# Spectral branch over the sequence in two halves, with seven more buffer pairs and runs of 13 key tiles

## The chip, the core and the metric

The kernel runs on one core of a Trainium2 chip. A core has a matrix engine (TensorE, PE in the profile, with PEld for its weight loads), a vector engine (VectorE, DVE), an activation engine (ScalarE, ACT), GpSimd (POOL) and SyncE (SP). Here SP computes nothing: it issues every DMA of the kernel, one after the other, and waits in its own order for what each DMA needs. The metric is the device time of one execution in microseconds (us). The kernel before took 1010.61 us, the median of three runs (1010.15 to 1011.03).

## The reference

Two independent branches read inputs of 2048 tokens by 448 features and are joined along the features, everything in float32:

```
a = einsum("bsd,ed->bse", x, dft_hid_re)
b = einsum("bsd,ed->bse", x, dft_hid_im)
y = einsum("ts,bse->bte", dft_seq_re, a) - einsum("ts,bse->bte", dft_seq_im, b)     # spectral branch
...
qkv = x @ wqkv                       # 16 heads of 28
p = softmax(q k^T * scale)
attention = (p v) @ wo
out = concatenate([y, attention])
```

The spectral branch is a transform along the features (448 by 448 matrices) and then one along the sequence (two 2048 by 2048 matrices). The attention branch is full softmax attention with 16 heads.

## The kernel before, in words

**Precision.** Most operands are split in two parts, a rounded high part and the rest (names ending in h and l, or hi and lo). A product is then three matmuls (high by high, low by high, high by low). ACT makes the high part, POOL or DVE the low part by a subtraction.

**The planner.** No order is written out by hand. The kernel describes tasks (`sch.add`, with helpers `pe`, `act`, `dve`, `pool`, `dma`) with an engine, a key (a due time in us), dependencies and the buffers they take; `Schedule.run` then plays through a modelled clock. Whenever an engine is free in the model it picks the ready task with the lowest key, and the instruction is emitted in that order. So the order on each engine is fixed when the kernel is built. On the chip an engine waits if its next instruction is not ready. The model of a DMA is in lines 284 to 291: besides fixed latencies, transfers pass one after another through a pipe of `FLOW_IN` = 310 (GB/s) in the first 20 us of the model (`T_IN`) and of `FLOW` after that (line 68), and at most eight DMAs are in flight (`LANES`).

**Fill and attention.** PE's work has two streams. The *fill* stream is a chain in a fixed order with two PSUM banks (`NFILL`): the projections of q and k (line 581 through `project`), the values (line 581 through `values`), the hidden transform (`hidden`, line 581 with weights in wd), and the sequence transform (`sequence`, line 718). Its keys (`fkey`) spread it evenly from the start to `T_FILL` = 1005. The *attention* stream takes the other six banks: for each head and each of 16 key tiles four score matmuls (line 865), each followed by an exponential on ACT (line 869) into half of a buffer *pair*. Its keys run from `T_ATT` = 56 to `T_END` = 935, so a key tile is due every 879 / 256 = 3.434 us. A head's first key tile has its own path (`first_tiles`, lines 806 to 839).

**Runs.** Exponentials times values (line 848, four matmuls for a key tile side by side in four groups of 32 columns) are not done one key tile at a time: `sums` gathers `run_size` key tiles, and when the exponentials of all of them are there PE does the whole run without a break. All pairs of the run stay taken until then: two pairs for each key tile. `RUN_AT` gives runs of 8 key tiles before a due time of 230 us and of 10 from there. Counted with 3.434 us for a key tile from 56 us, that is 7 runs of 8 (56 key tiles) and 20 of 10.

**Buffers.** `kept` holds 22 pairs of 4 KB for each partition. Three more are *lent* to it: they live in the place of a weight tile (tag wd) while no weights are there. A `Weights` object takes these three places back: from a due time on (`lent.until`, 50 us before the key of the hidden transform that needs the weights) nothing is lent any more, and the weights are converted into the place when the last lent pair is free. `big` is one tile of 57 KB for each partition. It holds x of the attention branch, split, until the last projection; then the spectral branch's a, split, for all 16 token tiles, and later -b in the same place.

**The spectral branch before.** `hidden(0)` makes a for all 16 token tiles (16 times 11 matmuls), `sequence(0)` multiplies dft_seq_re with it: 16 output tiles, each a sum over all 16 token tiles in one bank (48 matmuls, four pieces of dft_seq of 256 KB). DVE copies each result out (line 732), and it is stored to `y_d` in device memory. `hidden(1)` and `sequence(1)` do the same with b; here the stored y is loaded (line 735) once the third of the four pieces has begun (`Q_YO` = 2), DVE adds (line 736), and the sum is stored to `out`.

**The end.** After the last run, `out_of` normalises the last head through small DMAs to memory and back, the output projection (line 1003) follows in four chunks of 44 matmuls, copied out at line 431 and stored at line 1011. The rest of the fill runs beside it.

## Time and profile before

| | |
|---|---|
| median of three runs | 1010.61 us |
| profiled execution, its own time | 1010.71 us |
| span of its trace, first to last instruction | 1008.9 us |
| time outside the span | 1.81 us |
| ACT busy | 712.3 us (71%) |
| POOL busy | 366.9 us (36%) |
| DVE busy | 319.8 us (32%) |
| bytes moved by DMA | 124.84 MB |
| matmul records of line 718, line 581 with 448 columns, line 865, line 848 | 1536, 528, 960, 2048 |

A profile line such as `L848 PE MATMUL bank<-kept,v ... x64` names the line of the kernel, the engine, the operation, what is written and read, and the number of instructions. The matmuls of line 848 have float32 operands and leave two records each, so a key tile is eight records. Matmuls overlap: the duration of one record is longer than the step from one to the next, so the pace is read from the starts.

### The profile page before, as it was taken

Reading aid. Unit: us, or ns where it says so; the run is one execution under the profiler, and the core shown is the slowest. Engines: PE = TensorE matmul, PEld = TensorE weight load, DVE = VectorE, ACT = ScalarE, POOL = GpSimd, SP = SyncE. Lnnn points to the kernel's source line nnn. Section 1 sums busy time; section 2 is a strip of 40 time slices with the busy share of each in tenths; the row PEclk is TensorE's granted clock in tenths of the full one; section 3 lists DMA queues with packets and bytes.
Section 4 is the critical chain, followed back from the end, with each engine's and each line's share of the span. In section 5 each row is a group of like instructions: output and inputs, shape, how many; then the busy total and the mean of one; then the engine's idle time right before and its main releaser. Section 6 shows DMA issues by size and latency. Waiting matters only on the chain.

```text
span 1008.9 us, 15993 instructions
## 1 busy us (share of the span) xinstructions
PE 1001.6 (99%) x5634; PEld 735.3 (73%) x5634; DVE 319.8 (32%) x608; ACT 712.3 (71%) x1410; POOL 366.9 (36%) x338
## 2 busy tenths in 40 slices
PE   8999999999999999999999999999999999999998
PEld 7896667777766876686668667766786677667797
DVE  6362525251515042412314051614042152300112
ACT  6117979788767866796679778877786687668242
POOL 5112234353324323442325443434334252444530
PEclk9999999999999999999999999999999999999999
DMA  9797464323233333333233424332433343233463
GB/s 327 226 163 205 127 188 150 98 76 114 69 102 102 112 96 106 97 106 102 80 111 110 132 71 119 93 112 80 148 98 100 117 141 105 70 123 117 139 187 130
DMA packets 109908, 124.84 MB, mean 124 GB/s; under 512 B 48640, under 2 KB 61440, under 8 KB 109824
## 3 DMA queue, kind: packets, MB, share of 16 engines
q1 hardware_dynamic: 109824, 123.78, 40.8%
q8 instruction: 45, 0.74, 0.3%
q14 instruction: 39, 0.32, 0.1%
HBM read 89.92 MB, written 33.69 MB: 123 GB/s over the span
## 4 chain that ended last, share of the span: by engine, by line
PE 98%; DVE 1%; DMA 1%; SPq 0%; issue 0%; DVEq 0%
PE bank L718 31%; PE bank L865 23%; PE bank L848 22%; PE bank L581 17%; PE bank L1003 4%; PE bank L806 1%; DMA kept<-xb 1%; DVE big L427 0%; SPq L488 0%; SPq L559 0%; DVE kept L598 0%; DVE kept L736 0%; DVEq L427 0%
## 5 line engine op out<-in xcount | busy, mean ns | idle before, releaser
L869 ACT ACTIVATE kept<-bank 128x512 f32<-128x512 f32 x944 | 509.4, 673 | 90.7 <-PE bank L865 87.6
L530 POOL TENSOR_TENSOR wlo<-wraw,whi 128x512 fp32r<-128x512 f32 (+1 forms) x164 | 202.9, 1237 | 471.4 <-ACT whi L524 397.1
L865 PE MATMUL bank<-q,k 98*128 98x512 f32 x960 | 329.4, 398 | 0.0
L718 PE MATMUL bank<-big,whi 128*128 128x448 f32 x1024 | 310.9, 367 | 0.0
L848 PE MATMUL bank<-kept,v 128*32 128x512 f32 x2016 | 224.4, 593 | 0.0
L718 PEld LDWEIGHTS bank<-big,whi 128*128 128x128 f32 x1024 | 193.3, 189 | 29.2 <-issue 3.4
L865 PEld LDWEIGHTS bank<-q,k 98*128 98x128 f32 x960 | 180.4, 188 | 44.2 <-issue 11.7
L718 PE MATMUL bank<-big,wlo 128*128 128x448 f32 x512 | 188.3, 368 | 0.0
L848 PEld LDWEIGHTS bank<-kept,v 128*32 128x32 f32 x2016 | 63.5, 110 | 144.4 <-issue 142.3
L524 ACT ACTIVATE whi<-wraw 128x512 fp32r<-128x512 f32 x164 | 113.8, 694 | 21.0 <-PE bank L718 17.0
L718 PEld LDWEIGHTS bank<-big,wlo 128*128 128x128 f32 x512 | 96.7, 189 | 16.9 <-issue 5.9
L837 POOL TENSOR_TENSOR kept<-kept,mb 128x512 f32<-128x512 f32 x54 | 79.5, 1473 | 62.9 <-DVE mb L832 27.5
L581 PE MATMUL bank<-wd,whi 128*128 128x448 f32 x256 | 79.8, 367 | 0.0
L811 DVE STREAM_TRANSPOSE mb<-bank 128x512 f32<-128x512 f32 x64 | 45.8, 715 | 101.6 <-PE bank L806 87.9
L839 ACT ACTIVATE kept<-kept 128x512 f32<-128x512 f32 x64 | 45.1, 772 | 33.3 <-POOL kept L837 29.9
L581 PE MATMUL bank<-big,whi 128*128 128x512 f32 x175 | 60.1, 394 | 0.2 <-DVE kept L598 0.2
L832 DVE STREAM_TRANSPOSE mb<-am 128x512 f32<-128x512 f32 x64 | 45.4, 710 | 41.1 <-POOL kept L837 39.9
L810 ACT ACTIVATE kept<-bank 128x512 f32<-128x512 f32 x64 | 41.6, 672 | 22.5 <-PE bank L806 21.6
L581 PEld LDWEIGHTS bank<-wd,whi 128*128 128x128 f32 x256 | 48.3, 189 | 6.1 <-issue 0.8
L894 ACT ACTIVATE kept<-bank 128x512 f32<-128x512 f32 x16 | 9.5, 597 | 55.1 <-PE bank L848 55.1
L776 DVE TENSOR_REDUCE ok<-v 128x1 f32<-128x512 f32 x16 | 11.0, 686 | 115.5 <-DMA v<-vd 115.4
L736 DVE TENSOR_TENSOR kept<-bank,kept 128x448 f32<-128x448 f32 x15 | 9.3, 623 | 120.2 <-PE bank L718 106.0
(74 smaller groups left out, 745.8 us busy)
## 6 DMA issues: line engine op xcount, KB each, us to landing
wraw<-wre SPq DMA_DIRECT2D x64, 256.0 KB
wraw<-wim SPq DMA_DIRECT2D x64, 256.0 KB
qkd<-kept SPq DMA_DIRECT2D x40, 256.0 KB
wraw<-xa SPq DMA_DIRECT2D x32, 256.0 KB
k<-qkd SPq DMA_DIRECT2D x64, 112.0 KB
q<-qkd SPq DMA_DIRECT2D x64, 112.0 KB
out<-kept SPq DMA_DIRECT2D x31, 224.0 KB
kept<-xb SPq DMA_DIRECT2D x16, 256.0 KB
```

What stands on the lines that cost most here:

```text
L524: a = act(key + (0 if early else 1), lambda: nc.scalar.activation(self.hi.t, raw.t, AF.Copy), ACT_S, soon=SOON, deps=[ld], acq=[self.hi], ...
L530: b = sch.add(e, at, lambda g: eng[g].tensor_tensor(self.lo.t[:, :n], raw.t[:, :n], f32(self.hi.t)[:, :n], op=ALU.subtract), deps=[a], acq ...
L581: nc.tensor.matmul(o.t[:, :cols], w(), x(), start=(i == 0), stop=(i == n - 1))
L718: nc.tensor.matmul(o.t[:, :D], a.t[:, k, :], b[:, q * 4 + k, :], start=(q == 0 and k == 0 and j == 0), stop=(q == 3 and k == 3 and j == 2))
L810: made.append(act(key, lambda o=o, s=s: nc.scalar.activation(s.t, o.t, AF.Copy), deps=[m], use=[o, s.pair], lock=[o]))
L811: t = dve(key, lambda o=o, tm=tm: nc.vector.transpose(tm.t, o.t), 0.73, deps=[m], acq=[tm], use=[o], lock=[o], own=RAW_S)
L832: t = dve(key, lambda mb=mb, c=c: nc.vector.transpose(mb.t, f32(am.t)[:, c * NT:(c + 1) * NT].unsqueeze(2).to_broadcast([P, NT, 32])), 0.7 ...
L837: sh = sch.add({"DVE": 0.8, "POOL": POOL_2}, key, lambda e, s=s, mb=mb: eng[e].tensor_tensor(s.t, s.t, mb.t, op=ALU.add), deps=[t, made[c] ...
L839: shown.append(act(key, lambda s=s: nc.scalar.activation(s.t, s.t, AF.Exp, scale=SCALE), ACT_S, deps=[sh], use=[s.pair]))
L848: nc.tensor.matmul(o.t[c * VW:(c + 1) * VW, :], VT[h].t[:, kt // 4, kt % 4, :], tiles[c].t, start=(kt == 0), stop=(kt == NT - 1))
L865: m = pe(key, lambda e, o=o, q=q, kt=kt: nc.tensor.matmul(o.t, KT[h][kt // 4].t[:KM, kt % 4 * P:(kt % 4 + 1) * P], q.t[:KM, :], start=True ...
L869: es[h, kt].append(act(key - 20, lambda o=o, p=p: nc.scalar.activation(p.t, o.t, AF.Exp, scale=SCALE), deps=[m], use=[o, p.pair]))
```

## The change

The tokens of the spectral branch are taken in two halves of eight tiles. `big` becomes two tiles x0 and x1 of half its size, split by tokens. `hidden` and `sequence` run four times instead of twice: (part a, first half), (a, second half), (b, first), (b, second). The order of the hidden transform's 32 token tiles is the same; the sequence transform makes each of its 16 output tiles four times, each time from eight token tiles (24 matmuls, two pieces of 256 KB). a and -b of a half fit in x0 alone. The first of the four passes stores y by a copy as before, the second and third load y, add and store it again, the fourth loads, adds and stores to `out`. The load may now go out once the second of two pieces has begun (`Q_YO` = 1).

The hidden transform needs its weights four times. The first set is the held one as before; the other three are loaded and split anew, each taking the lent places back 50 us before its key.

x1 is free after the last projection. Its 28 KB hold seven more pairs (`more`, `held`), which join `kept` when the last matmuls that read x have been done: 29 pairs, and three lent ones.

`RUN_AT` changes to runs of 8 before 200 us and of 13 from there: 6 runs of 8 (48 key tiles) and 16 of 13. `FLOW` in the planner's model of a DMA goes from 200 to 300.

```diff
--- before.py
+++ after.py
@@ -34,10 +34,10 @@
 NKEPT = 22
 NKEYS = 4
 NFILL = 2
-Q_YO = 2
+Q_YO = 1
 N_WARM = 7
 N_FIRST = 3
-RUN_AT = ((0.0, 8), (230.0, 10))
+RUN_AT = ((0.0, 8), (200.0, 13))
 
 
 def run_size(t):
@@ -65,7 +65,7 @@
 RAW = 0.19
 RAW_S = 0.12
 LANES = 8
-FLOW, FLOW_IN = 200.0, 310.0
+FLOW, FLOW_IN = 300.0, 310.0
 T_IN = 20.0
 FIRST = {"PE": 1.4, "ACT": 2.0, "DVE": 2.0, "POOL": 1.4, "SP": 0.75}
 FLOW_AT = 1.4
@@ -355,7 +355,8 @@
     on_d = dram.tile([D, S], F32, name="ond")
 
 
-    big = new("big", [P, 2 * NT * D], F32R)
+    SIDE = 7 * S // 2
+    xs = [new(f"x{i}", [P, SIDE], F32R) for i in range(2)]
     lent = Lent(lambda: sb.tile([P, 2 * 4 * D], F32R, tag="wd", name="wd"),
                 lambda: [t[:, i] for t in (sb.tile([P, 3, 2, CH], F32, tag="wd", name="lent"),) for i in range(3)], 3)
     wraw = new("wraw", [P, 4, P], F32, 3, True)
@@ -377,6 +378,16 @@
     w_first.part(0)
     stage_s = Slots([w_first.tile[:, i * CH:(i + 1) * CH] for i in range(7)])
     kept_s.lent = lent
+    more, N_MORE = [], SIDE // (2 * CH)
+
+    def place_of(i):
+        if not more:
+            more.append(sb.tile([P, N_MORE, 2, CH], F32, tag="x1", name="more"))
+        return more[0][:, i]
+    held = [Slot(kept_s) for _ in range(N_MORE)]
+    for i, slot in enumerate(held):
+        slot.i = len(kept_s.tiles)
+        kept_s.tiles.append(lambda i=i: place_of(i))
     fill_s, bank_s = Slots(banks[:NFILL]), Slots(banks[NFILL:])
 
     class Half:
@@ -459,17 +470,23 @@
         return at + (f - HEAD) * (T_FILL - at) / (F_TOTAL - HEAD)
 
 
+    def x_part(i, s):
+        side, at = divmod(s.start, S // 2)
+        at += i * S // 2
+        return xs[side][:, at:at + s.stop - s.start]
+
     def x_h(k, s):
-        return big[:, k * S + s.start:k * S + s.stop]
+        return x_part(k, s)
 
     def x_l(k, s):
-        return big[:, (3 + k) * S + s.start:(3 + k) * S + s.stop]
+        return x_part(3 + k, s)
 
     def x_3(s):
-        return big[:, 6 * S + s.start:6 * S + s.stop]
-
-    ab_h = big[:, :NT * D].rearrange("p (t d) -> p t d", t=NT)
-    ab_l = big[:, NT * D:].rearrange("p (t d) -> p t d", t=NT)
+        return x_part(6, s)
+
+    NS = NT // 2
+    ab_h = xs[0][:, :NS * D].rearrange("p (t d) -> p t d", t=NS)
+    ab_l = xs[0][:, NS * D:].rearrange("p (t d) -> p t d", t=NS)
 
 
     def products(xh, xl, x3, wh, wl):
@@ -644,7 +661,8 @@
             pair = None if st else kept_s.slot()
             hi, lo = (stage_s.slot(), stage_s.slot()) if st else (Half(pair, 0), Half(pair, 1))
             own = [hi, lo] if st else [pair]
-            end = chain(key, seq, o, CH, [], w.own if first else [w.hi, w.lo], M512, own, parts)
+            end = chain(key, seq, o, CH, [], w.own if first else [w.hi, w.lo], M512,
+                        [*own, *(held if j == 6 and c == NC - 1 else ())], parts)
             key, out_key = (0.0, 11.0 if j == 0 else 25.0) if first else (key - 10, key - 10)
             stored(j, c, o, end, own, hi, lo, st, key, out_key)
         x_users.append(last[0])
@@ -663,7 +681,7 @@
                 seq = products(lambda k: lz(x_h, k, tok), lambda k: lz(x_l, k, tok), lambda: lz(x_3, tok),
                                lambda k: (lambda: w_first.h[:, k]), lambda k: (lambda: w_first.l[:, k]))
                 key = fkey(11, M448)
-                end = chain(key, seq, o, D, [], [], M448, [pair],
+                end = chain(key, seq, o, D, [], [], M448, [pair, *(held if c == NC - 1 and t == 3 else ())],
                             {3 * k: [xb_ready[c, k], ready[k], *ready[4:][:k // 3]] for k in range(4)}, v_last)
 
                 def put(o=o, vs=vs):
@@ -679,16 +697,16 @@
 
     y_stored = {}
 
-    def hidden(part, weights, ready, after):
+    def hidden(part, half, weights, ready, after):
         done = []
-        for st in range(NT):
+        for st in range(half * NS, (half + 1) * NS):
             key = fkey(11, M448)
             w = Piece(lambda st=st: xa[st], key - 9, "x")
             o = fill_s.slot()
             seq = products(lambda k, w=w: (lambda: w.hi.t[:, k]), lambda k, w=w: (lambda: w.lo.t[:, k]),
                            lambda w=w: (lambda: w.hi.t[:, 3]), lambda k: (lambda: weights.h[:, k]), lambda k: (lambda: weights.l[:, k]))
-            end = chain(key, seq, o, D, [*w.ready, *ready], [w.hi, w.lo], M448, weights.slots if st == NT - 1 else ())
-            hi, lo = ab_h[:, st, :], ab_l[:, st, :]
+            end = chain(key, seq, o, D, [*w.ready, *ready], [w.hi, w.lo], M448, weights.slots if st % NS == NS - 1 else ())
+            hi, lo = ab_h[:, st % NS, :], ab_l[:, st % NS, :]
             if part == 0:
                 a = act(key - 10, lambda o=o, hi=hi: nc.scalar.activation(hi, o.t[:, :D], AF.Copy), 0.43, soon=SOON, deps=[end, *after], use=[o])
                 b = dve(key - 10, lambda o=o, hi=hi, lo=lo: nc.vector.tensor_tensor(
@@ -701,22 +719,23 @@
             done.append(b)
         return done
 
-    def sequence(part, made):
+    def sequence(part, half, made):
         src = wim if part else wre
+        phase = 2 * part + half
         for tt in range(NT):
             o, pair = fill_s.slot(), kept_s.slot()
             yo = Half(pair, 0)
             begun = None
-            for q in range(4):
+            for q in range(2):
                 key = fkey(12, M448)
-                w = Piece(lambda tt=tt, q=q: src[tt, :, q * 4:q * 4 + 4, :], key - 13)
+                w = Piece(lambda tt=tt, q=half * 2 + q: src[tt, :, q * 4:q * 4 + 4, :], key - 13)
                 for i in range(12):
                     k, j = divmod(i, 3)
 
                     def emit(e, k=k, j=j, q=q, w=w, o=o):
                         a, b = ((w.hi, ab_h), (w.hi, ab_l), (w.lo, ab_h))[j]
                         nc.tensor.matmul(o.t[:, :D], a.t[:, k, :], b[:, q * 4 + k, :], start=(q == 0 and k == 0 and j == 0),
-                                         stop=(q == 3 and k == 3 and j == 2))
+                                         stop=(q == 1 and k == 3 and j == 2))
                     first = q == 0 and i == 0
                     deps = [last[0]]
                     if i == 0:
@@ -728,14 +747,15 @@
                     if i == 0 and q == Q_YO:
                         begun = last[0]
             key = key - 10
-            if part == 0:
+            if phase == 0:
                 b = dve(key, lambda o=o, yo=yo: nc.vector.tensor_copy(yo.t[:, :D], o.t[:, :D]), 0.53, deps=[last[0]], use=[o, pair])
                 y_stored[tt] = dma(key, lambda yo=yo, tt=tt: nc.sync.dma_start(y_d[tt], yo.t[:, :D]), deps=[b], use=[pair])
             else:
                 ld = dma(key - 15, lambda yo=yo, tt=tt: nc.sync.dma_start(yo.t[:, :D], y_d[tt]), deps=[y_stored[tt], begun], use=[pair])
                 b = dve(key, lambda o=o, yo=yo: nc.vector.tensor_tensor(yo.t[:, :D], o.t[:, :D], yo.t[:, :D], op=ALU.add), 0.53,
                         deps=[last[0], ld], use=[o, pair])
-                dma(key, lambda yo=yo, tt=tt: nc.sync.dma_start(out[tt * P:(tt + 1) * P, 0:D], yo.t[:, :D]), deps=[b], use=[pair])
+                to = out[tt * P:(tt + 1) * P, 0:D] if phase == 3 else y_d[tt]
+                y_stored[tt] = dma(key, lambda yo=yo, to=to: nc.sync.dma_start(to, yo.t[:, :D]), deps=[b], use=[pair])
 
 
     def rows_of(dst, once, r0, c0, c1):
@@ -934,16 +954,18 @@
         project(j, weights_of(j), range(NC))
     key = fkey(0, 0)
     staged = [d for j in range(N_FIRST, 5) for c in range(NC) for d in qk_done[j, c]]
-    made = hidden(0, w_first, load_w(w_first, lambda k: wd[:, k, :D], key - 10, after=[v_last[0], *staged]), x_users)
-    a_last = last[0]
-    sequence(0, made)
-    y_last = last[0]
-    key = fkey(0, 0)
-    w_b = Weights(lent)
-    lent.until.append(key - 50)
-    made = hidden(1, w_b, load_w(w_b, lambda k: wd[:, k, D:], key - 10, after=[a_last]), [y_last])
-    b_last = last[0]
-    sequence(1, made)
+    made = hidden(0, 0, w_first, load_w(w_first, lambda k: wd[:, k, :D], key - 10, after=[v_last[0], *staged]), x_users)
+    h_last = last[0]
+    sequence(0, 0, made)
+    for part, half in ((0, 1), (1, 0), (1, 1)):
+        y_last = last[0]
+        key = fkey(0, 0)
+        w_n = Weights(lent)
+        lent.until.append(key - 50)
+        ready = load_w(w_n, lambda k, part=part: wd[:, k, part * D:(part + 1) * D], key - 10, after=[h_last])
+        made = hidden(part, half, w_n, ready, [y_last])
+        h_last = last[0]
+        sequence(part, half, made)
     for h in range(H):
         head_loads(h)
     for h in range(H):
@@ -953,7 +975,7 @@
 
     w_out = Weights(lent)
     lent.until.append(T_END - 80)
-    wo_ready = load_w(w_out, lambda k: wo[:, k], T_END - 40, after=[b_last])
+    wo_ready = load_w(w_out, lambda k: wo[:, k], T_END - 40, after=[h_last])
     HF = CH // 2
     starts = []
     for n, c in enumerate(range(NC)):
```

## The prediction

> **What bounds the kernel now.** I read the page's shares and slices first, then the chain of waits, then PE's own timeline.
>
> ```profile
> span 1008.9 us, 15993 instructions
> ...
> PE 1001.6 (99%) x5634; PEld 735.3 (73%) x5634; DVE 319.8 (32%) x608; ACT 712.3 (71%) x1410; POOL 366.9 (36%) x338
> ...
> PEclk9999999999999999999999999999999999999999
> ...
> PE 98%; DVE 1%; DMA 1%; SPq 0%; issue 0%; DVEq 0%
> ```
>
> PE is busy for 1001.6 of 1008.9 us at the full granted clock, and the chain that ended last is 98% PE. A busy matrix engine need not be a fast one, so the second look is at its pace, and at what a run costs beyond its key tiles.
>
> ```profile
> 92.80 0.39 PE L581 MATMUL bank<-big,wlo 128*128 128x512 f32 x1
> 93.03 0.40 PE L865 MATMUL bank<-q,k 98*128 98x512 f32 x1
> ...
> 93.60 7.07 PE L848 MATMUL bank<-kept,v 128*32 128x512 f32 x64
> 100.60 0.50 PE L865 MATMUL bank<-q,k 98*128 98x512 f32 x1
> ...
> 283.04 0.40 PE L865 MATMUL bank<-q,k 98*128 98x512 f32 x1
> 283.27 0.57 PE L718 MATMUL bank<-big,whi 128*128 128x448 f32 x2
> 283.78 8.79 PE L848 MATMUL bank<-kept,v 128*32 128x512 f32 x80
> 292.50 0.47 PE L718 MATMUL bank<-big,wlo 128*128 128x448 f32 x1
> 292.81 0.36 PE L718 MATMUL bank<-big,whi 128*128 128x448 f32 x1
> 293.01 0.40 PE L865 MATMUL bank<-q,k 98*128 98x512 f32 x1
> ```
>
> Starts follow each other by 0.23 us after a matmul of 512 columns (92.80 to 93.03, 283.04 to 283.27) and 0.20 us after one of 448 (292.81 to 293.01): PE issues without gaps. A run of 8 key tiles occupies PE for 7.00 us (93.60 to 100.60), one of 10 for 8.72 (283.78 to 292.50). So a key tile is (8.72 - 7.00) / 2 = 0.86 us, and a run has a constant of 7.00 - 8 x 0.86 = 0.12 us. On the way in, the two matmuls from 283.27 should take 0.40 us and take 0.51: another 0.11. **One run costs about 0.23 us** beside its work.
>
> Two chains could take PE's place as the limit: the attention stream by way of ACT, and DMA. ACT in the 20 runs of 10, and in the 19 stretches between them (first two columns: stretch, its length; each engine's busy time follows):
>
> ```profile
> 283.78:292.50 8.72, 8.72 (x81) 2.50 (x81) 0.00 (x0) 1.68 (x4) 0.08 (x1) 1.00 0.27 86
> ...
> sum 174.42, PE 174.42 PEld 49.95 DVE 34.42 ACT 45.47 POOL 43.25; mean PE 8.72 PEld 2.50 DVE 1.72 ACT 2.27 POOL 2.16
> ```
>
> ```profile
> 292.50:318.90 26.40, 26.40 (x127) 22.97 (x123) 10.67 (x22) 24.21 (x49) 10.50 (x8) 1.00 0.36 104
> ...
> sum 480.46, PE 480.46 PEld 416.33 DVE 150.96 ACT 445.43 POOL 207.30; mean PE 25.29 PEld 21.91 DVE 7.95 ACT 23.44 POOL 10.91
> ```
>
> The 71% of the page hide two regimes. Between runs ACT is busy for 23.44 of 25.29 us (93%), and 1.85 us idle is little. During a run no scores are made: ACT works off the full banks for 2.27 us and then stands still. So the attention stream goes about as fast as ACT lets it, and the fill is what PE does while ACT catches up.
>
> The end shows how near the two streams are:
>
> ```profile
> 994.71 9.13 PE L1003 MATMUL bank<-wd,q 128*128 128x448 f32 x44
> 1003.68 0.36 PE L718 MATMUL bank<-big,wlo 128*128 128x448 f32 x1
> 1003.88 0.57 PE L718 MATMUL bank<-big,whi 128*128 128x448 f32 x2
> 1004.29 0.37 PE L718 MATMUL bank<-big,wlo 128*128 128x448 f32 x1
> ...
> 1004.69 0.62 DVE L736 TENSOR_TENSOR kept<-bank,kept 128x448 f32<-128x448 f32 x1 [9.47 <-PE bank L718]
> ...
> 1002.20 2.58 SPq L1011 DMA_DIRECT2D out<-kept  x2
> 1005.35 0.33 SPq L738 DMA_DIRECT2D out<-kept  x1
> ```
>
> The last store of the attention branch is issued by 1004.78 (1002.20 + 2.58), that of the spectral branch by 1005.68, both of 224 KB. Fill ends the kernel, and attention has 0.9 us of slack.
>
> **The change part by part.**
>
> *Matmuls.* 4 x 8 x 11 hidden and 4 x 16 x 24 sequence matmuls replace 2 x 16 x 11 and 2 x 16 x 48: the same 352 and 1536. Nothing.
>
> *Runs.* 48 / 8 + 208 / 13 = 6 + 16 = 22 instead of 7 + 20 = 27. Five fewer at 0.23 us: **-1.1 us**. The bounds are 5 x 0.12 = 0.6, if the way in overlapped anyway, and 1.2.
>
> The Trainium skill, "TensorEngine Tiling (Array Packing)", Key Properties, says that a change of tiling mode drains the array, and "TensorE: Matmul & The Clock Gate", Single matmul latency, has a constant of 166 ns beyond the columns for a lone warm matmul. Estimated from these pages, two drains for each run would be 0.33 us and five runs 1.7 us; the rows say 0.23, and I use them.
>
> *Partial sums.* 32 more loads and 32 more stores of 224 KB, and 32 adds.
>
> ```profile
> L736 DVE TENSOR_TENSOR kept<-bank,kept 128x448 f32<-128x448 f32 x15 | 9.3, 623 | 120.2 <-PE bank L718 106.0
> ...
> 939.50 0.62 SPq L897 DMA_DIRECT2D sm<-kept  x1
> ...
> 941.44 0.25 DVE L898 RECIPROCAL sm<-sm 128x16 f32<-128x16 f32 x1 [1.20 <-DMA sm<-kept]
> ...
> 955.03 0.35 SPq L735 DMA_DIRECT2D kept<-yd  x1
> ...
> 959.08 0.62 DVE L736 TENSOR_TENSOR kept<-bank,kept 128x448 f32<-128x448 f32 x1 [7.89 <-PE bank L718]
> ```
>
> The adds are 32 x 0.623 = 20 us on a DVE that is 32% busy, and the 14.7 MB are 12% more than the 124.84 moved at a mean DMA share of 41%. What could show on PE is a bank that comes free late. A load of y takes between 1.94 us (8 KB, from issue to its user) and 4.05 us (224 KB, issue to an add that waited for PE). Where PE does fill alone, a tile of 24 matmuls takes 24 x 0.20 = 4.9 us and the load may go at its middle, 2.4 us before its end; the add then starts between 0.5 us early and 1.6 us late. The bank is wanted only a whole tile later, 4.9 us: that tile is the cover. Without cover, at the very last tile, it costs up to 1.6 us; there the 9 us of line 1003 stood before the last five matmuls, so I take 0 and keep 1.6 for the range.
>
> *Weights.* Two more sets:
>
> ```profile
> L508 ACT ACTIVATE wd<-wraw x16: 568/584/676, 22.9 to 897.9; 128x448 fp32r<-128x448 f32 x16
> ...
> L427 POOL TENSOR_TENSOR wd<-wraw,wd x16: 1139/1152/1165, 23.6 to 899.4; 128x448 fp32r<-128x448 f32 x12, 64x448 fp32r<-64x448 f32 x4
> ```
>
> Eight conversions are 8 x 0.584 = 4.7 us of ACT, and eight subtractions 9.2 us of POOL, which is idle for over 60%. They wait for the three lent pairs. A pair taken just before a run lives until the next run, now 13 x 3.434 = 44.6 us, against 34.3 before; the places close 50 us and the weights are wanted some 10 us before the key. That leaves the conversions late by a few us where a run begins right at the closing. I take 0: the run that frees the pairs itself keeps PE busy for 13 x 0.86 + 0.12 = 11.3 us, longer than four conversions and subtractions.
>
> *Pairs.* A run of 13 holds 26. 29 + 3 lent leave 3 to 6 over, where 22 + 3 less 20 left 2 to 5: the same room, so no gain and no loss.
>
> *Attention's pace.* In attention's cycle a run adds its 0.12 us and the 1.85 us of ACT's idle time after it, and hands 2.27 us of ACT's work to PE's run. Five fewer runs therefore lengthen attention by 5 x (2.27 - 1.85 - 0.12) = 1.5 us, and the conversions by 0 (in runs, where ACT is idle for 174.42 - 45.47 = 129 us) to 4.7. On the other side the last run is 13 instead of 10: when its scores are complete PE has 2.6 us less of line 848 behind it, so PE gets there earlier. I take these as cancelling, within the 0.9 us of slack; the bound is a rival below.
>
> *The planner's DMA rate* moves no instruction by itself; it reorders them. PE's early loads are the place:
>
> ```profile
> 0.00:20.00 20.00, 16.91 (x71) 13.68 (x72) 11.59 (x16) 14.29 (x26) 13.24 (x26) 1.00 0.88 311
> ...
> 40.00:60.00 20.00, 20.00 (x99) 18.39 (x98) 8.22 (x31) 0.60 (x1) 0.00 (x0) 1.00 0.87 159
> 60.00:80.00 20.00, 20.00 (x96) 17.65 (x96) 14.71 (x40) 6.75 (x13) 5.66 (x6) 1.00 0.98 172
> ...
> 83.79 0.38 SPq L773 DMA_DIRECT2D v<-vd  x1
> ```
>
> From 40 to 80 us the DMA engines are 87 to 98% busy with only 159 to 172 GB/s. The plan believed 200 and will believe 300. The bytes of those 40 us, (159 + 172) x 20 = 6.62 MB, are 33 us of transfer by the old belief and 22 by the new: up to 11 us too early. But the values are stored as fast as PE makes them, and PE's pace is planned rightly; and there is a reserve: v goes out at 83.79 and its first run starts at 93.60. I take 0.
>
> The Trainium skill, "DMA: Bandwidth & Descriptors", Specifications, asks for transfers of at least 512 bytes for the full rate, and the stores to vd here have rows of 128 bytes. The trace agrees: 311 GB/s at a share of 0.88 in the first 20 us, 172 at 0.98 among the vd stores. By that rule 300 is a wrong belief for just this window, which speaks against this part.
>
> *Sum:* 1010.71 (the profiled execution) - 1.1 = **1009.6 us**. The median of the runs lies 0.1 lower than that execution; the difference is left out.
>
> **The rivals.**
>
> *Attention ends the kernel.* Runs delay it by 1.5 us and the conversions by up to 4.7, 6.2 together; less 0.9 of slack that is 0.6 to 5.3 us over the present end, 1011.3 to 1016.0. For it: ACT's 93% between runs, and an output projection that follows the last run at a fixed distance. Against it: 19 x 1.85 = 35 us of idle time that could absorb it.
>
> *PE stops for early loads (the other side, slower).* Place: the first heads, 40 to 100 us. Mechanism: PE's fixed order puts scores or the first run ahead of loads that the chip moves at 165 GB/s, not 300. It decides once the plan's lead is over the reserve: 9.8 us for v less a landing of 2 to 4 us, so 6 to 8. At the full lead of 11 PE stops for 3 to 5 us, and nothing returns that: 1009.6 + 4 = 1013.6. Against it: the pace of the values, above.
>
> *The last y is late:* up to 1.6 us less the 1.1 gained, near 1010.4.
>
> *More than the runs is gained:* attention starts earlier because the plan trusts the loads, and the small stops of PE go. Outside the first 20 us (3.1 idle, which the change does not touch) and the last 4.6 us little is left to win: 1008.3.
>
> **How the numbers follow.** Forecast 0.42 (1008.9 to 1010.6), attention 0.27, early loads 0.20, late y 0.04, more gained 0.07. A measurement of this kernel tells about 0.2%, 2.0 us: faster is under 1008.6, slower over 1012.6. Faster: 0.07 and 0.03 of the forecast's edge, 0.10. Slower: 0.14 of attention's cases, 0.18 of the loads', 0.02 elsewhere, 0.34. Same: 0.56. Range: 1008.3 to 1015.0.
>
> **What would show it.** 22 runs, those of 13 near 11.3 us; PE without idle time after 20 us; a last store from line 738; ACT between runs not over 95%. Wrong if the last store is line 1011's by a us or more, if PE waits before line 806, 865 or 848 between 50 and 110 us, or if line 581's first matmul of a half waits for wd.

## The result and the profile after

The changed kernel takes 1022.12 us, the median of five runs (1020.13 to 1024.16), against 1010.69 us (1010.15 to 1011.20) for the kernel before in the same rounds. The ratio is 1.0113, with a 95% interval of 1.0099 to 1.0127: 11.4 us slower. The forecast of 1009.6 us and its range up to 1015.0 were both wrong.

The profiled execution is the slowest of the five, 1024.16 us with a span of 1022.6, so the traces differ by 13.7 us where the medians differ by 11.4. Its page, shares and slices first:

```profile
span 1022.6 us, 16185 instructions
...
PE 1008.4 (99%) x5634; PEld 739.6 (72%) x5634; DVE 336.0 (33%) x638; ACT 715.2 (70%) x1418; POOL 376.3 (37%) x350
...
PEclk9989999999999999999999999999999999999999
...
PE 93%; DMA 2%; ACT 2%; DVE 1%; SPq 1%; issue 0%; POOL 0%; POOLq 0%; DVEq 0%; ACTq 0%
```

PE is still 99% busy, and the same 5634 records now take 6.8 us more "busy" time. Two small signs are on the page: one slice, the third of 25.6 us each, has a granted clock below nine tenths, and the chain has fallen from 98% PE to 93%. The view of waits on PE names the place (total, times, longest, in us):

```profile
PE bank L885 <- POOL q L855: 5.5, 1, 5.5
```

Line 885 is the score matmul (865 before), line 855 the row copy of a head's first key tile (835 before). The longest wait is one of 5.5 us, on GpSimd. Before, the first score matmul of this kind in the PE timeline stood later, and it did not wait:

```profile
70.47 0.43 PE L865 MATMUL bank<-q,k 98*128 98x512 f32 x1
```

The same stretch of the changed kernel, all engines in order of start (start, duration, engine, line; in brackets the idle time before and what ended it):

```profile
60.83 1.32 SPq L765 DMA_DIRECT2D q<-qkd  x1
...
61.30 0.40 PE L885 MATMUL bank<-q,k 98*128 98x512 f32 x1
...
62.69 0.61 SPq L540 DMA_DIRECT2D wraw<-wqkv  x1
...
67.12 0.99 POOL L547 TENSOR_TENSOR wlo<-wraw,whi 128x384 fp32r<-128x384 f32 x1 [7.26 <-ACT whi L541]
68.18 0.61 POOL L855 CAST q<-mb 1x512 fp32r<-1x512 f32 x1
...
68.84 0.79 PE L885 MATMUL bank<-q,k 98*128 98x512 f32 x1 [5.51 <-POOL q L855]
```

And from the chain of waits, what stands between the load and the subtraction (start, length, what):

```profile
62.20 0.39 SPq L766
...
62.69 3.65 DMA wraw<-wqkv
...
66.36 0.64 ACT whi L541
```

With the belief in 300 GB/s the plan puts head 0's scores at 61.30 instead of 70.47, 9.2 us earlier. The second query chunk's scores need its row copy. That copy is a small GpSimd instruction, and in GpSimd's fixed order it stands behind the subtraction of a piece of projection weights (line 547), which waits for ACT's cast, which waits for the piece's load. SP issues that load at 62.69: in its fixed order two loads of q stand ahead of it (1.32 us for the issue at 60.83, 0.39 for the next). Neither v nor the scores' own operands were the late load: **a weight piece was, by way of an in-order queue.**

The stop is not the whole price. The view of windows, cut here into stretches of 3.41 us (stretch, length; busy time of PE, PEld, DVE, ACT, POOL; granted clock; DMA share; GB/s):

```profile
64.92:68.33 3.41, 0.00 (x0) 0.00 (x0) 0.00 (x0) 1.15 (x2) 1.14 (x2) 1.00 0.99 217
68.33:71.74 3.41, 2.90 (x8) 2.54 (x9) 2.03 (x5) 2.12 (x4) 2.99 (x6) 0.50 1.35 227
71.74:75.16 3.42, 3.42 (x11) 2.98 (x10) 1.30 (x4) 1.16 (x2) 1.13 (x2) 0.50 1.02 201
75.16:78.57 3.41, 3.41 (x18) 3.03 (x17) 1.11 (x5) 1.65 (x5) 0.00 (x0) 1.00 0.52 92
```

After one stretch with no matmul the granted clock is 0.50 for exactly two stretches, 6.83 us. PE works in 2.90 + 3.42 = 6.3 us of them at half speed and loses 3.2 us: a stretch that is busy throughout holds 11 matmuls at 0.50 and 18 at 1.00. So this one event costs 5.5 + 3.2 = 8.7 us. PE counts as busy in the slow part, so these 3.2 us do not lower the page's 99%; they are about half of the 6.8 us of added busy time.

The rest is seen at the end (PE timelines; first fence before, second after):

```profile
936.41 2.32 PE L848 MATMUL bank<-kept,v 128*32 128x512 f32 x18
```

```profile
947.46 1.03 PE L868 MATMUL bank<-more,v 128*32 128x512 f32 x6
...
1016.56 0.36 PE L737 MATMUL bank<-x,wlo 128*128 128x448 f32 x1
...
1016.96 0.62 DVE L755 TENSOR_TENSOR kept<-bank,kept 128x448 f32<-128x448 f32 x1 [4.24 <-PE bank L737]
```

The last run ends at 948.49 (947.46 + 1.03) instead of 938.73: 9.8 us later, of which the stop and its clock are 8.7 and five fewer runs -1.1 by the prediction's price; 2.2 are left, which would be smaller stops of PE; they are a remainder and not read from rows. Behind that the kernel takes another 3.9 us more: PE's last matmul starts at 1016.56 and ends 5.7 us before the span does, where it was 4.2 (1004.29 + 0.37 to 1008.9), which is 1.5; the other 2.4 lie between.

### The profile page after: what moved, and what is told of

It is laid out like the page before. It is cut to its first block, busy times and chain, and to the rows that moved or that the text cites. A ratio compares the mean times of both kernels' runs of the same rounds, so it can differ in the third digit from the quotient of the medians.

```text
span 1022.6 us, 16185 instructions
## 1 busy us (share of the span) xinstructions
PE 1008.4 (99%) x5634; PEld 739.6 (72%) x5634; DVE 336.0 (33%) x638; ACT 715.2 (70%) x1418; POOL 376.3 (37%) x350
## 4 chain that ended last, share of the span: by engine, by line
PE 93%; DMA 2%; ACT 2%; DVE 1%; SPq 1%; issue 0%; POOL 0%; POOLq 0%; DVEq 0%; ACTq 0%
PE bank L737 29%; PE bank L868 22%; PE bank L885 21%; PE bank L598 15%; PE bank L1025 3%; PE bank L826 1%; PE bank L633 1%; ACT kept L889 1%; DMA kept<-ond 0%; DMA wraw<-wd 0%; DMA wraw<-wqkv 0%; SPq L765 0%; DMA kept<-xb 0%; ACT whi L541 0%; DMA q<-qkd 0%
## 5 line engine op out<-in xcount | busy, mean ns | idle before, releaser
L889 ACT ACTIVATE kept<-bank 128x512 f32<-128x512 f32 x732 | 416.3, 701 | 76.2 <-PE bank L885 74.0
L737 PE MATMUL bank<-x,whi 128*128 128x448 f32 x1024 | 312.4, 367 | 0.0
L737 PEld LDWEIGHTS bank<-x,whi 128*128 128x128 f32 x1024 | 193.4, 189 | 27.3 <-issue 1.7
L868 PE MATMUL bank<-kept,v 128*32 128x512 f32 x1580 | 209.0, 593 | 0.0
L737 PE MATMUL bank<-x,wlo 128*128 128x448 f32 x512 | 188.2, 368 | 0.0
L889 ACT ACTIVATE more<-bank 128x512 f32<-128x512 f32 x220 | 129.8, 696 | 9.6 <-PE bank L885 8.7
L737 PEld LDWEIGHTS bank<-x,wlo 128*128 128x128 f32 x512 | 96.7, 189 | 15.2 <-issue 4.2
L868 PE MATMUL bank<-more,v 128*32 128x512 f32 x452 | 87.1, 592 | 0.0
L857 POOL TENSOR_TENSOR kept<-kept,mb 128x512 f32<-128x512 f32 x43 | 63.8, 1484 | 34.7 <-DVE mb L852 28.5
L598 PE MATMUL bank<-x,whi 128*128 128x512 f32 x175 | 58.7, 393 | 0.0
L830 ACT ACTIVATE kept<-bank 128x512 f32<-128x512 f32 x58 | 38.0, 674 | 22.5 <-PE bank L826 22.3
```

Of the source, the lines that this page charges most:

```text
L598: nc.tensor.matmul(o.t[:, :cols], w(), x(), start=(i == 0), stop=(i == n - 1))
L737: nc.tensor.matmul(o.t[:, :D], a.t[:, k, :], b[:, q * 4 + k, :], start=(q == 0 and k == 0 and j == 0), stop=(q == 1 and k == 3 and j == 2))
L830: made.append(act(key, lambda o=o, s=s: nc.scalar.activation(s.t, o.t, AF.Copy), deps=[m], use=[o, s.pair], lock=[o]))
L857: sh = sch.add({"DVE": 0.8, "POOL": POOL_2}, key, lambda e, s=s, mb=mb: eng[e].tensor_tensor(s.t, s.t, mb.t, op=ALU.add), deps=[t, made[c] ...
L868: nc.tensor.matmul(o.t[c * VW:(c + 1) * VW, :], VT[h].t[:, kt // 4, kt % 4, :], tiles[c].t, start=(kt == 0), stop=(kt == NT - 1))
L889: es[h, kt].append(act(key - 20, lambda o=o, p=p: nc.scalar.activation(p.t, o.t, AF.Exp, scale=SCALE), deps=[m], use=[o, p.pair]))
```

## The experiments

The first theory: the planner's rate of 300 is the main cost, through the stop at 63 us. Its rival: the halves and the longer runs are (their weights, partial sums and pairs), and the stop is where PE would have waited anyhow. After these, the runs ask what a stop costs, and where the rest of the loss is.

**The rate alone, taken away from the change and given to the kernel before.**

```diff
--- after.py
-FLOW, FLOW_IN = 300.0, 310.0
+FLOW, FLOW_IN = 200.0, 310.0
```

> The changed kernel with the planner's DMA rate back at 200; halves, seven pairs, runs of 13 and Q_YO stay. Theory F (the rate puts PE's scores ahead of the projection weights, PE stops for 5.9 us at 63 us, and the clock granted after the stop is 0.72 for some 11 us, 3 us more): no stop, 9 us or more less, 1009.5 to 1013 us. Rival H (the halves cost it: reloaded weights, partial sums, later attention): the stop may go, but the kernel stays over 1016 us.

```diff
--- before.py
-FLOW, FLOW_IN = 200.0, 310.0
+FLOW, FLOW_IN = 300.0, 310.0
```

> The kernel before with the planner's DMA rate at 300 and nothing else. Theory F: a stop of some 6 us between 55 and 75 us with a clock under 1 behind it, 1018 to 1022 us. Rival H: within 3 us of 1010.7.

Measured: the change with 200 takes 1015.34 us (1015.01 to 1015.68), ratio 1.0047 (1.0034 to 1.0061); the kernel before with 300 takes 1019.07 (1018.85 to 1021.13), ratio 1.0085 (1.0072 to 1.0099). Windows of the change with 200:

```profile
62.90:68.90 6.00, 6.00 (x31) 5.54 (x30) 4.95 (x18) 0.63 (x1) 1.02 (x1) 1.00 1.12 186
```

Waits on PE, and windows, of the kernel before with 300:

```profile
PE bank L865 <- POOL q L835: 5.5, 1, 5.5
```

```profile
62.80:68.70 5.90, 0.42 (x3) 0.03 (x2) 0.03 (x1) 1.15 (x2) 1.60 (x2) 0.93 0.92 190
68.70:75.00 6.30, 6.30 (x17) 5.53 (x18) 3.02 (x8) 3.27 (x6) 3.73 (x6) 0.52 1.14 198
```

The stop, the line it waits for and the half clock come and go with this one number. It costs 1022.12 - 1015.34 = 6.8 us in the change and 8.3 us alone in the kernel before, as the theory had it. But the change with 200 lies between the two expectations, 1009.5 to 1013 and over 1016: 4.6 us remain without the rate.

**Where the rate does its harm.** The rate of 300 from 90 us of the plan on only, and the rate of 300 everywhere with the 256 KB stores of v counted as 512 KB:

```diff
--- after.py
-                        flow = max(flow, at + 0.4) + size / (FLOW if now > T_IN else FLOW_IN)
+                        flow = max(flow, at + 0.4) + size / (FLOW if now > 90.0 else 200.0 if now > T_IN else FLOW_IN)
```

> The changed kernel with the planner's rate at 200 up to 90 us of its clock and at 300 after that. Theory F with the early window alone to blame: no early stop, 1009.5 to 1013 us, within 1 us of the kernel at 200 all through. If 300 also does harm later (the small stops at 338, 403, 790 to 802, 841 and 980 us): 2 to 4 us slower than that one. Rival H: over 1016 us.

```diff
--- after.py
-                    vs.t.rearrange("p (h x) -> p h x", h=H)), extra=1.0, deps=[b], use=[pair]))
+                    vs.t.rearrange("p (h x) -> p h x", h=H)), size=512, extra=1.0, deps=[b], use=[pair]))
```

> The changed kernel with the rate of 300, but the planner counts each store to vd (rows of 128 bytes) as 512 KB instead of 256, so that it believes 1.7 us for one. The instructions are the same, only their order can differ. If the vd stores are what the belief gets wrong: the early stop shrinks to under 2 us and the time is 1010 to 1014 us. If the loads of q and k or the weights are wrong by themselves: the stop stays at 4 us or more and the time over 1017 us.

Measured: 1017.12 us (1014.79 to 1018.01), ratio 1.0062 (1.0048 to 1.0076), for the first, and 1015.43 (1013.66 to 1016.16), ratio 1.0044 (1.0030 to 1.0058), for the second. Neither trace has the stop at 63 us; the longest wait on PE of the second is one of 1.6 us in the output projection, near the end. So 5.0 of the 6.8 us lie in the first 90 us; the other 1.8, for the rate later on, fall between the 1 and the 2 us expected, and the intervals do not tell them from nothing. And 300 is not wrong for the kernel as a whole: corrected for the stores of v alone, it costs no more than 200 does, though the second run too stays above the 1010 to 1014 us expected of it.

What the second run changed is the order on GpSimd, not the early scores (timelines of PE and of GpSimd):

```profile
60.78 0.40 PE L885 MATMUL bank<-q,k 98*128 98x512 f32 x1
...
65.62 0.62 POOL L855 CAST q<-mb 1x512 fp32r<-1x512 f32 x1 [2.08 <-DVE mb L852]
70.59 1.01 POOL L547 TENSOR_TENSOR wlo<-wraw,whi 128x384 fp32r<-128x384 f32 x1 [4.35 <-ACT whi L541]
```

Its first scores stand at 60.78, even earlier than the 61.30 of the change, but on GpSimd four row copies, the last at 65.62, come ahead of the subtraction that waits for a weight piece. **Early scores alone do not stop PE.** In the three traces with the early stop, a row copy stands behind a subtraction that is still waiting; no run changes this order and nothing else. The early start is worth little by itself: the first run of line 868 begins at 87.64, 6 us earlier than the 93.60 of the kernel before, and the last one still ends at 939.35, not before 938.73.

**How much trust is too much.** The kernel before with a rate of 250:

```diff
--- before.py
-FLOW, FLOW_IN = 200.0, 310.0
+FLOW, FLOW_IN = 250.0, 310.0
```

> The kernel before with the planner's rate at 250. If the harm sets in when the plan's lead is over the reserve of the early loads: either no early stop and 1010 to 1012 us (250 still within the reserve), or a shorter stop of 1 to 4 us with a low clock behind it, 1013 to 1017. If it grows in proportion to the rate: about half of what 300 cost, 1015 us.

Measured: 1018.46 us (1017.64 to 1018.65), ratio 1.0078 (1.0064 to 1.0092). Waits on PE, the first score matmul in its timeline, and windows:

```profile
PE bank L865 <- POOL q L835: 3.8, 1, 3.8
...
61.21 0.40 PE L865 MATMUL bank<-q,k 98*128 98x512 f32 x1
```

```profile
68.32:71.73 3.41, 0.48 (x3) 0.12 (x1) 0.87 (x4) 1.61 (x4) 0.85 (x1) 1.00 1.06 269
71.73:75.14 3.41, 2.53 (x6) 2.05 (x7) 0.00 (x0) 2.76 (x7) 2.58 (x5) 0.50 1.33 183
75.14:78.56 3.42, 3.42 (x10) 2.92 (x10) 0.00 (x0) 1.94 (x4) 0.00 (x0) 0.50 1.09 189
```

All the expectations, 1017 us at most, were too low: half the step in the rate brings as much as the whole step, 8.3 us over the kernel before of the same rounds (1010.13 here, 1010.73 there). The scores come just as early, at 61.21, where 300 has them at 61.17. The wait is shorter, 3.8 us, but PE did next to nothing for a whole stretch, and the half clock comes in full length: (2.53 + 3.42) / 2 = 3.0 us. The next stretch, from 78.56, is at 1.00 again.

**What a stop costs by itself.** In the kernel before, at head 7 (424 us), the row copy is done 33 times on GpSimd; everything else stays.

```diff
--- before.py
-            row.append(sch.add({"DVE": 0.7, "POOL": 0.7}, key, lambda e, q=q, mb=mb: eng[e].tensor_copy(q.t[96:97, :], mb.t[96:97, :]),
-                               deps=[t], use=[mb, q]))
+            late = h == 7 and c == 0
+
+            def put_row(e, q=q, mb=mb, n=33 if late else 1):
+                for _ in range(n):
+                    eng[e].tensor_copy(q.t[96:97, :], mb.t[96:97, :])
+            row.append(sch.add({"POOL": 0.7} if late else {"DVE": 0.7, "POOL": 0.7}, key, put_row, deps=[t], use=[mb, q]))
```

> The kernel before, in which GpSimd makes one row copy of the eighth head 33 times instead of once (32 x 0.6 = 19 us more on GpSimd at 424 us, which the planner does not know of), so that PE must stop for some us between 430 and 450 us, far from the early DMA load. If a stop of PE is what lowers the granted clock (theory C): a clock under 1 for some 10 us after the stop, and the kernel longer by the stop and about half as much again. If the low clock belonged to the early window or to its DMA traffic: a clock of 1.00 after the stop and the kernel longer by the stop alone.

Measured: 1031.82 us (1031.09 to 1032.75), ratio 1.0213 (1.0197 to 1.0229), 21.05 us over the 1010.77 of its rounds. The copies keep GpSimd busy for 22.79 us from 423.48 on. Waits on PE, and windows:

```profile
PE bank L869 <- ACT lent L873: 18.3, 1, 18.3
```

```profile
431.57:434.98 3.41, 0.00 (x0) 0.00 (x0) 0.00 (x0) 0.00 (x0) 3.09 (x6) 1.00 0.01 2
434.98:448.63 13.65, 0.00 (x0) 0.00 (x0) 1.14 (x3) 0.01 (x1) 11.76 (x18) 0.50 0.00 0
448.63:452.05 3.42, 2.26 (x6) 1.77 (x6) 2.19 (x4) 3.42 (x7) 1.75 (x2) 0.50 0.00 0
452.05:455.46 3.41, 3.41 (x10) 2.79 (x9) 0.08 (x1) 3.19 (x8) 2.51 (x2) 0.50 0.18 50
455.46:458.88 3.42, 3.42 (x17) 3.01 (x17) 0.62 (x1) 3.37 (x7) 1.13 (x1) 1.00 0.37 123
```

The cost is the stop, 18.3, plus 2.7; the "half as much again" of the expectation was far too much. PE worked 2.26 + 3.41 = 5.7 us at half clock, which is 2.8. So a stop lowers the clock far from the early loads too, at a DMA share near 0. No idle time elsewhere returns any of it, though ACT has plenty: PE has no second order to fall back on. The clock's part is about the same for stops of 3.8, 5.5 and 18.3 us (3.0, 3.2, 2.8).

**What remains without the rate: the length of the runs.** The change with the rate and the runs of before (10 key tiles from 230 us), and the kernel before with runs of 8 throughout, 32 runs in place of 27:

```diff
--- after.py
-RUN_AT = ((0.0, 8), (200.0, 13))
+RUN_AT = ((0.0, 8), (230.0, 10))
...
-FLOW, FLOW_IN = 300.0, 310.0
+FLOW, FLOW_IN = 200.0, 310.0
```

> The changed kernel with the planner's rate at 200 and the runs of before (8, then 10 from 230 us): the halves, their partial sums and three reloads, and the seven pairs, without the long runs. Theory R (what is left over 1010.7 us at a rate of 200, 4.6 us, comes from the halves: conversions of reloaded weights that wait behind exponentials, and a later end): 1014 to 1018 us, five more turns making it about 1 us slower than with runs of 13. Rival L (it comes from the long runs, during which ACT stands still): 1010 to 1012 us.

```diff
--- before.py
-RUN_AT = ((0.0, 8), (230.0, 10))
+RUN_AT = ((0.0, 8), (2000.0, 10))
```

> The kernel before with runs of 8 all through: 32 runs instead of 27. By the price of a turn from the trace, 0.23 us for each run, PE loses 1.1 us: 1011.8 us, if PE's own work sets the end. By attention's pace the same five runs more would shorten attention by 1.5 us, which gains nothing while fill ends the kernel: the same 1011.8. If turns cost nothing: 1010.7.

Measured: the halves with runs of 10 take 1013.85 us (1012.86 to 1014.02), ratio 1.0030 (1.0018 to 1.0043). The runs of 13, made to save time, cost 1015.34 - 1013.85 = 1.5 us. The intervals of the ratios overlap, but no execution of the one is as fast as the slowest of the other (1015.01 and 1014.02). The expectation that the halves are the cause had it the other way, 1 us slower with runs of 10; its rival had 1012 us at most, so the halves have a part of their own. What PE's weight loads wait for suggests why the long runs cost; first the change with a rate of 200, then the same with runs of 10:

```profile
PEld bank L885 <- ACT kept L889: 7.1, 29, 0.8
...
PEld bank L885 <- ACT more L889: 1.6, 8, 0.3
```

```profile
PEld bank L885 <- ACT kept L889: 4.2, 21, 0.3
...
PEld bank L885 <- ACT more L889: 0.8, 3, 0.3
```

With runs of 13, scores wait for ACT for 8.7 us in all instead of 5.0. A longer run leaves ACT idle longer at a time, and it cannot catch up so well between runs. These 3.7 us of weight loads that wait are not all stops of PE, but they are of the size that is needed, 1.5 + 1.1 for the runs that were saved; that they are the whole cause is argued from the size. Too few spare pairs would be another cause, but neither trace has a wait of line 889 for line 868, which frees them.

How much of it is attention is read from the start of the first run to the end of the last. The last rows are, with a rate of 200 and then with runs of 10 too:

```profile
939.45 1.04 PE L868 MATMUL bank<-more,v 128*32 128x512 f32 x8
```

```profile
937.82 1.04 PE L868 MATMUL bank<-more,v 128*32 128x512 f32 x8
```

That is 846.7 us with runs of 13 (93.75 to 940.49), 846.0 with runs of 10 (92.82 to 938.86) and 845.1 in the kernel before (93.60 to 938.73). These are single executions, and two of one plan (the halves with runs of 10, with and without the branch of the last experiment) differ by 0.4.

The kernel before with 32 runs takes 1013.34 us (1012.34 to 1013.92), ratio 1.0026 (1.0016 to 1.0035), where 1011.8 at most was expected. Its span, 1012.0 us, is 3.1 us longer, and part of this is not the runs:

```profile
1005.89 0.37 PE L718 MATMUL bank<-big,wlo 128*128 128x448 f32 x1
```

Its last matmul ends at 1006.26, 5.7 us before the span's end, 1.5 us more than before; the view of waits on SP has 1.5 us there for the last store to land. That leaves 1.6 us for five runs, 0.3 each where the prediction had 0.23. From the first run to the end of the last it is 846.6 us (93.69 to 940.32), 1.5 more than before.

**The weights' reload.** In the change with a rate of 200 the third reload shows as a stop (timelines of PE and of ACT):

```profile
786.92 1.58 PE L885 MATMUL bank<-q,k 98*128 98x512 f32 x6
789.01 1.48 PE L885 MATMUL bank<-q,k 98*128 98x512 f32 x3 [0.51 <-ACT kept L889]
...
790.81 0.37 PE L598 MATMUL bank<-wd,whi 128*128 128x448 f32 x1
...
786.20 0.62 ACT L525 ACTIVATE wd<-wraw 128x448 fp32r<-128x448 f32 x1
```

From 786.92 to 790.81 PE makes ten matmuls in 3.89 us, 1.6 more than at 0.23 each. No run covers the conversions here: they stand between exponentials, on an ACT that is busy for 6.73 of the 6.9 us before. Conversions 40 us earlier in ACT's order, first in the change with a rate of 200, then in the one with runs of 10 too:

```diff
--- after.py, with FLOW = 200
-                    deps=[ld, *after], use=[raw, *own])
+                    soon=0.0 if w is w_first else SOON, deps=[ld, *after], use=[raw, *own])
```

> The changed kernel at a rate of 200, with the key of the reloaded weights' conversions on ACT 40 us earlier (as the fill's other ACT work has it), so that they no longer come after exponentials. Theory R: the stops between 787 and 791 us go (1.6 us), also those near 394, 1012.5 to 1014 us. If the reloads are not what stops PE there: 1015.3 us as without the edit.

> Halves, seven pairs, a rate of 200, runs of 8 and 10, and the reloaded weights' conversions 40 us earlier in key: the best of the parts so far. The stops near 789 us (0.8 us) should go: 1013.0 us. It stays over the 1010.7 of before by the longer end if theory T holds.

Measured: 1014.41 us (1014.13 to 1014.47), ratio 1.0037 (1.0024 to 1.0051), 0.9 less than without, between the two expectations; the stretch from 786.68 to 789.43 now holds eight matmuls in 2.75 us, so 0.9 of the 1.6 us stay:

```profile
786.68 2.92 PE L885 MATMUL bank<-q,k 98*128 98x512 f32 x8
789.43 0.37 PE L598 MATMUL bank<-wd,whi 128*128 128x448 f32 x1
```

With runs of 10 the same edit makes it worse: 1014.73 us (1014.05 to 1015.38), ratio 1.0042 (1.0028 to 1.0056), 0.9 more than without it, where 1013.0 was expected. One edit of a key reorders the plan, and short waits appear at other places: here scores wait for ACT for 8.1 us (6.4 + 1.7) instead of 5.0. The reload costs about 1 us in one of these plans; it is not a constant.

**The end.** The end after the last matmul takes 4.2 to 6.4 us in the traces so far, and it is not one thing. Both kernels end with a branch over a path for large scores, which is never taken up on these inputs. Here that path and the branch are left out, in the kernel before and in the halves with runs of 10 and a rate of 200:

```diff
--- both
-    fine = nc.values_load(fi, min_val=0, max_val=1)
-    with tc.If(fine == 0, preferred_fallthrough_block=False):
-        any_scores(tc, qk_d, v_d, on_d, wo, out, kt_s.tiles, q_s.tiles, v_s.tiles, kept_s.tiles, banks, new)
+    nc.values_load(fi, min_val=0, max_val=1)
```

> The kernel before without the fallback for large scores at its end (the branch over it and its code are left out; the flag is still computed and loaded). From the last matmul to the end of the span it takes 4.6 us with the fallback. Theory T (behind the last branch the engines wait for their next instructions, for a time that differs from build to build, and the kernel before happens to wait little): 1009.5 to 1010.7 us. Rival: the branch costs nothing anywhere, 1010.7.

> Halves, seven pairs, a rate of 200 and runs of 8 and 10, without the fallback, as the run beside it. With it this kernel took 1013.85 us, 6.8 us of them from the last matmul to the end. Theory T: 1 to 2.5 us less, 1011.3 to 1012.8, and at most 2.5 us over the kernel before without the fallback. Rival (the longer end belongs to the stores of the halves): 1013.8 us, still 3 us apart.

Measured: the kernel before gains nothing, 1010.53 us (1009.33 to 1011.47), ratio 1.0001 (0.9992 to 1.0010). The halves go from 1013.85 to 1012.13 (1011.16 to 1013.12), ratio 1.0017 (1.0008 to 1.0026). The last matmuls, of the halves with the branch (span 1011.4 us) and then without (span 1010.1 us):

```profile
999.76 5.27 PE L1025 MATMUL bank<-wd,q 128*128 128x448 f32 x25
```

```profile
999.66 6.28 PE L1025 MATMUL bank<-wd,q 128*128 128x448 f32 x30
```

With the branch 1011.4 - 1005.03 = 6.4 us lie behind the last matmul, without it 1010.1 - 1005.94 = 4.2, as much as in the kernel before. So some 2 us of the end hang on the branch in these builds, and not in the one of before. SP's last branch and its first instruction behind it show where (first the kernel before, then the halves with the branch; the times are the first and the last start):

```profile
L1028 SPq COMPARE_BRANCH  x2: 38/46/53, 1006.6 to 1006.7; - x2
...
L1128 SPq EVENT_SEMAPHORE  x14: 17/28/28, 1007.2 to 1008.8; - x14
```

```profile
L1050 SPq COMPARE_BRANCH  x2: 38/46/53, 1006.9 to 1007.0; - x2
...
L1150 SPq EVENT_SEMAPHORE  x14: 17/28/28, 1009.8 to 1011.4; - x14
```

SP goes on 0.5 us after its last branch in the kernel before and 2.8 us after it in the halves. Why the builds differ was not tried. Less than the 2.2 us arrives in the time: the runs shorten by 1.7 us by the medians and by 1.1 against the kernel before of their own rounds (1010.77 and 1010.13), and the time outside the span grows from 1.6 us to 2.2.

No version here beats the kernel before: the best, the halves without rate, long runs or branch, is 1012.13, and without its branch the kernel before takes 1010.53.

## Why the prediction was wrong, point by point

The loss of 11.4 us divides, by medians, into 6.8 for the rate (1022.12 to 1015.34), 1.5 for the length of the runs (1015.34 to 1013.85) and 3.1 for the halves themselves (1013.85 to 1010.7), of which 1.1 to 1.7 go with the branch.

- **The planner's DMA rate, taken as 0, is the step that failed.** "It reorders them" was right, and so were the place, the line and the direction of its rival (the first heads, a wait before line 865). What failed is the reason for the 0, a lead set against a reserve, and the reserve read from one operand, v, which had 9.8 us to spare. The runs show an order in its place: a row copy stands on GpSimd behind a subtraction that waits for a late piece of projection weights, which stops PE for 5.5 us and leaves it at half clock for 3.2 us more; 6.8 us in the change and 8.3 in the kernel before. Lead and reserve do not decide it. The lead of the scores is 9.2 us at 300, where up to 11 had been worked out; at 250 the same arithmetic gives 33.1 - 26.5 = 6.6 us and the trace has 9.3; and with the stores of v counted double it is 9.7 and PE does not stop. The prediction set beside this part a rule of the Trainium skill ("DMA: Bandwidth & Descriptors", Specifications), at least 512 bytes for the full rate, by which 300 is a wrong belief for the stores of v. Counting just these stores double takes the stop away, which agrees with it; that they were what the plan had wrong is not shown, since the rate of 200 up to 90 us does the same.
- **The rival's price, 3 to 5 us, left out the clock.** The stop itself was 5.5 us; 3.2 came on top. "Nothing returns that" was right.
- **Runs, -1.1 us:** the mechanism was right. There are 22 runs, those of 13 take 11.3 us as said, and five more runs cost 1.6 us where 1.1 was forecast. But the saving did not arrive, because of the next term.
- **Attention's pace, taken as cancelling, was mis-sized.** Attention became 1.6 us longer without the rate, 0.7 with the length of the runs and 0.9 with the halves. The 1.5 worked out for five runs was more than the 0.7, but nothing cancelled either part. In the kernel before, five more runs made attention 1.5 us longer, where the formula has it shorter, so the formula does not hold there. The profile of before had the warning: ACT at 93% between runs. It took the form of many short waits of PE more than that of a late last store.
- **The weights' reload, taken as 0:** wrong for the third set, which met no run and cost about 1.6 us in one plan. "The run that frees the pairs itself keeps PE busy" holds only where a run begins near the closing of the places.
- **Partial sums, 0:** right. The last add starts 0.04 us after the last matmul (1016.92 to 1016.96), so its y was there; the rival of a late last y did not happen. (The 24 x 0.20 us of the cover are 4.8, not 4.9; nothing hangs on it.)
- **The end had no term at all.** It took 1.5 us more in the change.
- **More gained through an earlier attention:** this did not happen. In the run with scores 9.7 us earlier and no stop at 63 us, the last run ends at 939.35, no earlier than before.

## What to carry to other kernels

A number in a planner's model is a change to the order of every queue: before it is raised, look in the stretch where the model is furthest from the trace, and there look at the order on each engine that works in a fixed order: which small instruction, needed at once, comes to stand behind one that waits for a load? The slack of the operands themselves does not show this. Price a stop of the matrix engine as its length plus what the clock takes away behind it. A matrix engine that is 99% busy can still have lost time; compare how many matmuls equal stretches hold, and the granted clock of short windows.

## What the hardware showed that was not expected

**The half clock comes in whole stretches.** In the three traces whose windows are cut at 3.41 us it lasted a multiple of that: 6.83 after stops of 3.8 and 5.5 us, and 20.48 (434.98 to 455.46) around the long one. It begins at the end of a stretch in which PE did almost nothing (0.00 to 0.48 us), and ends after a stretch in which PE worked throughout; a stretch with 2.26 to 2.90 us of work does not end it. The Trainium skill, "TensorE: Matmul & The Clock Gate", Part 1, describes a window of about 3.4 us that runs freely, half clock after an idle one and full clock after a busy one. The traces agree. What they add is the price of one stop. One such stretch full of work at half clock would cost 1.7 us, half of 3.41; here it was 2.8 to 3.2, because the stretch in which PE resumed was not full and another at half clock followed. The price is not a constant: one of the five executions of the change has a mean clock of 0.998 where the other four have 0.996, so its half clock was shorter, and it took 1020.13 us, 2.0 less than the median.

**Short stops left the clock alone.** From 20 us on to the last matmul the granted clock of every trace is under 1.00 only behind the stops of 3.8, 5.5 and 18.3 us; waits of PE of 1.6 us and less left it at 1.00. No run has a stop between these lengths, so where the limit lies is not shown.

**The end of a program can depend on code that is never run.** The end behind the last matmul was 6.4 us in the halves and 4.2 in these without the branch, with the difference right behind SP's last branch. Not every long end is of this kind: in the kernel before with 32 runs it was 5.7 us, and there SP goes on 0.5 us after its last branch (1008.3 to 1008.8) and waits for a store. The Trainium skill, "Runtime: NRT & Kernel Launch", Instruction fetch mechanics, says that a taken branch to code outside the pages at hand waits for a fetch. The trace of the halves has two loads on an instruction queue (q14) between 1007.1 and 1009.7 us, while SP stands; that SP waits for them is not shown, since the kernel before has one within its 0.5 us too.
